# Four modulation vectors summed over the partitions: TensorE products against a GpSimd all-reduce

## The chip, the cores and the metric

The kernel runs on one core of a Trainium2 chip. The metric is the device time of one execution in microseconds; the time of a kernel is the median of its runs. Beside it stands one profiled execution, taken by the hardware profiler. Engines are named as the profile names them: PE is TensorE (PEld its weight loads), DVE is VectorE, ACT is ScalarE, POOL is GpSimd, SP is SyncE, which here issues most DMAs.

## The reference

A transformer block with adaptive layer norm: attention, then a gated MLP that mixes over the sequence. Six vectors of 448 elements come from one small product and scale and shift the two halves.

```
mod = silu(c) @ w_mod            # c is 1 x 448, w_mod 448 x (6 x 448)
sa, ca, ga, sb, cb, gb = mod     # six vectors of 448
h = layernorm(x) * (1 + ca) + sa
x = x + ga * attention(h, wqkv, wo)          # 16 heads of 28, 2048 rows
h = layernorm(x) * (1 + cb) + sb
z = gelu(h @ w_in); z1, z2 = halves of z; z2 = layernorm(z2)
x = x + gb * ((z1 * (w_sp @ z2 + b_sp)) @ w_out)
```

All data are single precision.

## The kernel before

Each large product is made in three terms: an operand is split into a part rounded to fp32r ("hi") and its remainder ("lo"), and hi x hi, hi x lo and lo x hi are summed in PSUM. The work goes in stages whose order is written out by hand; a semaphore waits wherever a tile, a buffer or a bank isn't free. Each engine, and the SP queue of DMA issues, works through its own instructions in the order of the program.

- **Start and projections (to some 83 us).** The rows of x go in four groups `g` of 512. For each group: `ln_transpose` (L104) transposes the normalised rows on PE, ACT scales and shifts them into `hfull`, rounds them into `hT`, and DVE subtracts to make the remainders; `v_tile` (L323) makes V; `qk_unit` (L329) makes 128 columns of Q or K for one group in 11 products, rounds the result into `qh`, subtracts for `ql`, and `qk_store` (L352) sends both to DRAM through SP. `qh`, `ql` and `qf` have two buffers each.
- **Preparation of the heads (group 3, L563 to L599).** `pads` (L572) fills parts of `kst` and `qst` for heads 0, 1 and 2, on DVE and POOL; `load_head` (L580) brings a head's Q and K back from DRAM through SP.
- **The ramp (L856 to L879).** The 18 remaining `qk_unit` calls run with the first products of the row maxima (`mt`, `m_mm`, L636) among their own. Here a unit is evacuated by ACT into `qf`, rounded into `qh`, and POOL subtracts for `ql` (L341 to L346). The units turn over three of the seven PSUM banks of the ring (L827 to L830), the `mt` products over the other four. The first six units are those of m = 4 for groups 0 to 3 and of m = 1 for groups 1 and 2.
- **Attention proper (to some 870 us), then the MLP.** PE makes scores, weighted sums and their like without a break.

**The vectors.** `sa` and `ca` are made at the start and the change doesn't touch them. The other four come in pairs, (ga, sb) as pair 1 and (cb, gb) as pair 2. `mod_acc` (L228) multiplies the rows of `w_mod` by silu(c) on DVE and adds them up in `acc`, 128 partitions by two times 448: what is left is a sum over the 128 partitions. `mod_split` (L245) makes hi and lo of `acc`: ACT rounds, and POOL (pair 1) or DVE (pair 2) subtracts. `mod_sum` (L256) multiplies each by a matrix of ones on PE, so that the sum stands in all 128 partitions of a bank. `mod_bc` (L263) copies it out (ga, gb); `mod_col` (L266) takes partition 0 as a row, adds 1 for cb, sends the row to DRAM and reads it back as columns by three DMAs, all through SP (sb, cb).

Pair 1 is accumulated among the products of group 1, split within group 3's `ln_transpose` (L552) and summed after `v_tile(11)` (L605, L606). Pair 2 is accumulated among the products of group 2, split after `v_tile(12)` (L595) and summed after `v_tile(15)` (L615, L616), just ahead of the ramp. In POOL's order, `pads` for heads 0, 1 and 2 come between the two pairs' sums, and the first `ql` of the ramp follows the second.

Of the kernel before, what the change touches and what calls it, by code (L numbers as in the profile page):

```python
# [1 line left out]

# [5 lines left out]

F32 = mybir.dt.float32
F32R = mybir.dt.float32r  # L10
AF = mybir.ActivationFunctionType
ALU = mybir.AluOpType
# [4 lines left out]
S, D, H, DH, FH = 2048, 448, 16, 28, 896  # L17
# [16 lines left out]
def tile_adaln_mha_gmlp(ctx, tc, x, wqkv, wo, w_in, w_spT, b_sp, w_out, cT, w_mod0, w_mod, out):  # L34
    nc = tc.nc
    ctx.enter_context(tc.manual_schedule())
    pe, dve, act, pool, sp = nc.tensor, nc.vector, nc.scalar, nc.gpsimd, nc.sync
# [3 lines left out]
    scr = ctx.enter_context(tc.tile_pool(name="scr", bufs=1, space=DRAM))  # L41
# [15 lines left out]
    cols = {}  # L57
    for nm in ("sa", "ca", "sb", "cb"):
        cols[nm] = const.tile([128, 4], F32, name=f"col_{nm}")
    bcs = {"gb": const.tile([128, D], F32, name="bc_gb")}  # L60
# [5 lines left out]
    def hview(heap, off, a, b):  # L66
        return heap[:, off : off + a * b].rearrange("p (a b) -> p a b", b=b)

    hT = [hview(heapD[g // 2], g % 2 * 3584, 7, 512) for g in range(NG)]
# [11 lines left out]
    def sub(eng, dst, a, hi):  # L81
        eng.tensor_tensor(out=dst, in0=a, in1=hi.bitcast(F32), op=ALU.subtract)  # L82
# [60 lines left out]
    stage = stg.enter_context(tc.tile_pool(name="stage", bufs=2, side="right"))  # L143
# [6 lines left out]
    e1 = early.enter_context(tc.tile_pool(name="e1", bufs=2))  # L150
    e2 = late_e.enter_context(tc.tile_pool(name="e2", bufs=1, side="right"))

    wv = e2.tile([128, 8, D], F32R, name="wv")
    ones_r = e2.tile([128, 128], F32R, name="ones_r")
    dve.memset(ones_r.bitcast(F32), 1.0)
    wms, xts, raws = {}, {}, {}


# [2 lines left out]
    def bank(name):  # L161
        k = mode[0](name) if mode[0] else banks[0]
        banks.remove(k)
        banks.append(k)
        return ring.tile([128, 512], F32, name=name, tag=f"b{k}")
# [52 lines left out]
    pc = bank("pc")  # L218
# [7 lines left out]
    accs = {}  # L226

    def mod_acc(pair, k):  # L228
        if k == 0:
            accs[pair] = e2.tile([128, 2, D], F32, name="acc")  # L230
        wm, acc = wms.pop((pair, k)), accs[pair]
        if k < 3:
            wm = wm.rearrange("r (p n) -> r p n", p=2)
        if k == 0:
            dve.tensor_scalar(out=acc, in0=wm, scalar1=silu[:, 0:1], scalar2=None, op0=ALU.mult)
        elif k < 3:
            dve.scalar_tensor_tensor(out=acc, in0=wm, scalar=silu[:, k : k + 1], in1=acc, op0=ALU.mult, op1=ALU.add)
        else:
            half_rows(wm, [acc[:, part] for part in range(2)])

    def half_rows(wm, outs):
        for part, o in enumerate(outs):
            dve.scalar_tensor_tensor(out=o, in0=wm, scalar=silu[:, 3 + part : 4 + part], in1=o, op0=ALU.mult, op1=ALU.add)

    def mod_split(pair, eng, pool_l, tag_l, bufs_l):  # L245

        acc = accs.pop(pair)
        accs[pair] = []
        for part in range(2):
            h = stage.tile([128, 512], F32R, name="acc_h", tag="qf")[:, :D]  # L250
            l = pool_l.tile([128, D], F32R, name="acc_l", tag=tag_l, bufs=bufs_l)
            act.activation(h, acc[:, part, :], AF.Copy)
            sub(eng, l, acc[:, part, :], h)
            accs[pair].append((h, l))

    def mod_sum(pair, part):  # L256

        pc = bank("pc")
        for i, a in enumerate(accs[pair][part]):
            pe.matmul(pc[:, :D], ones_r, a, start=i == 0, stop=i == 1)  # L260
        return pc[:, :D]

    def mod_bc(nm, pair, part):  # L263
        dve.tensor_copy(bcs[nm], mod_sum(pair, part))

    def mod_col(nm, pair, part, plus1):  # L266
        row, dst = e2.tile([1, D], F32, name="row"), scr.tile([D], F32, name=f"{nm}_scr")
        dve.tensor_scalar(out=row, in0=mod_sum(pair, part)[0:1], scalar1=plus1, scalar2=None, op0=ALU.add)
        sp.dma_start(dst.rearrange("(o n) -> o n", o=1), row)
        for r, e, c in ((0, 128, slice(0, 3)), (0, 64, slice(3, 4)), (64, 128, slice(3, 4))):  # L270
            src = dst[0:384] if e - r == 128 else dst[384:D]
            sp.dma_start(cols[nm][r:e, c], src.rearrange("(c p) -> p c", p=e - r))

    mv1, xn1 = {}, {}
# [13 lines left out]
    def ln_norm(g, ts):  # L288
        mv, rs = mv1[g]
        for t in ts:  # L290
            xn = e1.tile([128, 512], F32, name="xn", bufs=4)
            dve.tensor_scalar(
                out=xn[:, :D],
                in0=xts.pop(4 * g + t),
                scalar1=mv[:, t, 0:1],
                scalar2=rs[:, t : t + 1],
                op0=ALU.subtract,
                op1=ALU.mult,
            )
            act.activation(xn[:, D:], xn[:, 384:D], AF.Copy)  # L300
            xn1.setdefault(g, []).append(xn)
# [21 lines left out]
    def v_tile(kt):  # L323
        v_copy(*v_mm(kt))
# [212 lines left out]
    def ln_step(g, t):  # L537
        ln_stat(g, (t,))
        if t % 2:
            ln_rs(g, t - 1, t + 1)  # L540

    def ln_next(g):

        if g + 1 < NG:
            ln_transpose(
                xn1.pop(g), e1, hT[g], cols["ca"], cols["sa"], (act,) * 4, (dve,) * 4, None,
                lambda c: ln_step(g + 1, (0, 2, 1, 3).index(c)),
            )
            ln_norm(g + 1, range(4))
        else:  # L550
            ln_transpose(
                xn1.pop(g), e1, hT[g], cols["ca"], cols["sa"], (act,) * 4, (dve,) * 4, None, lambda c: c == 2 and mod_split(1, pool, e1, "wm", 4)  # L552
            )

    ln_next(1)
    load_x(3, sp)
    qk_unit((1,), 0)
# [4 lines left out]
    for g in range(1, NG):  # L562
        if g == 3:  # L563
            early.close()
            stk = att.enter_context(tc.tile_pool(name="stk", bufs=1))
            kq = [[stk.tile([128, S], F32R, name=f"{n}st{i}") for n in "kq"] for i in range(3)]
            kst, qst = [a[0] for a in kq], [a[1] for a in kq]
            npool = att.enter_context(tc.tile_pool(name="npool", bufs=2))
            late_s = ExitStack()
            late_l = late_s.enter_context(tc.tile_pool(name="late_l", bufs=2))  # L570

            def pads(i, eng):  # L572

                dve.memset(kst[i][64:128, :].bitcast(F32), 0.0)
                eng.memset(qst[i][64:128, :].bitcast(F32), 0.0)
                pool.memset(kst[i][64:86, :].bitcast(F32), 1.0)

            pads(0, dve)

            def load_head(h, c0=0, c1=S):  # L580
                k, q = kst[h % 3], qst[h % 3]
                if h > 2:
                    sp.dma_start(q[84:86, :].bitcast(F32), q[86:88, :].bitcast(F32))
                for r0, i in ((0, 0), (56, 1), (28, 0)):
                    sp.dma_start(k[r0 : r0 + 28, c0:c1].bitcast(F32), qk_scr[i][D + h * DH : D + (h + 1) * DH, c0:c1])
                for r0, i in ((0, 0), (28, 1), (56, 0)):
                    sp.dma_start(q[r0 : r0 + 28, c0:c1].bitcast(F32), qk_scr[i][h * DH : (h + 1) * DH, c0:c1])

            load_head(0, 0, 1536)
            for m in (0, 3):  # L590
                qk_unit((m,), g)
            load_head(0, 1536, S)
        v_tile(4 * g)
        if g == 3:
            mod_split(2, dve, late_l, "acc_l", 2)  # L595
        v_tile(4 * g + 1)
        if g == 3:
            pads(1, pool)
            pads(2, pool)  # L599
        if g + 1 < NG:  # L600
            ln_next(g + 1)
        for k in range(2):
            v_tile(4 * g + 2 + k)
            if g == 2 and k == 1:
                mod_bc("ga", 1, 0)  # L605
                mod_col("sb", 1, 1, 0.0)  # L606
            if g == 1 or g == 2 and k == 1:
                mod_acc(g, k if g == 1 else 0)
        if g < 3:
            for k, m in enumerate((0, 3)):  # L610
                qk_unit((m,), g)
                mod_acc(g, 3 - g + k)
            if g == 2:
                mod_acc(g, 3)
    mod_col("cb", 2, 0, 1.0)  # L615
    mod_bc("gb", 2, 1)  # L616
    late_s.close()
    late_e.close()


# [368 lines left out]
    h = H - 1  # L989
# [247 lines left out]
    acc = {}  # L1237
# [264 lines left out]
```

## Time and profile before

| what | value |
|---|---|
| median of 3 runs | 1396.14 us (1395.83 to 1396.7) |
| the profiled execution's own time | 1396.56 us |
| its span, first to last instruction | 1394.8 us |
| DMA queues with data | q1: 181.42 MB, q10: 4.30 MB, both hardware |
| instruction queues | q8: 0.92 MB, q14: 0.37 MB |
| granted TensorE clock, mean | 0.999 |

How to read it: the page's first part gives the busy time of each engine, its fourth the chain of work that ended last, its fifth groups of instructions by line (`out<-in`, count, busy time, mean in ns, and after the second bar the engine's idle time ahead of them with what ended it). A timeline row has the start and length in us, engine, line, operation, tiles and count. A row of a stretch (`a:b`) has its length, then the busy time and instructions of PE, PEld, DVE, ACT and POOL, then the granted clock, the DMA engines' busy share and GB/s. A row of the chain has the start, the length and what was on it.

### The profile page before, as it was taken

To read this page: it belongs to the slowest core of one execution; us is meant where nothing else is said; L and a number is where in the kernel's file an instruction comes from. 1 tells how busy PE (TensorE), PEld (TensorE's weight loads), DVE (VectorE), ACT (ScalarE), POOL (GpSimd) and SP (SyncE) were. 2 spreads that over 40 slices of the span, in tenths; PEclk is the share of its full clock that TensorE was granted. 3 is DMA by queue.
4 is the path that set the end of the run, shared out by engine and by line. 5 is a ranking of instruction groups with operands and counts; after the bars stand their busy time and mean duration, and the time that the engine had idled before them with its cause. 6 is when DMAs were issued, how large, how long until landed. Compare 5 with 4: busy or idle time off the path is not lost.

```text
span 1394.8 us, 20314 instructions
## 1 busy us (share of the span) xinstructions
PE 1389.4 (100%) x7170; PEld 989.0 (71%) x7170; DVE 1033.3 (74%) x1769; ACT 780.4 (56%) x1498; POOL 279.1 (20%) x279
## 2 busy tenths in 40 slices
PE   9999999999999999999999999999999999999998
PEld 8888655555555555555555555988998888888888
DVE  7898888888888888888888851750477655668573
ACT  6623677776666777777777778363244444334211
POOL 2134212222224143323200021000132430000000
PEclk9999999999999999999999999999999999999999
DMA  8464644665465556555323002434103333445453
GB/s 281 140 176 177 192 111 154 176 169 159 148 174 165 163 166 188 161 159 157 105 68 78 20 18 75 165 116 140 46 8 108 112 113 107 143 143 159 144 175 105
DMA packets 99489, 187.01 MB, mean 134 GB/s; under 512 B 17656, under 2 KB 29434, under 8 KB 96842
## 3 DMA queue, kind: packets, MB, share of 16 engines
q1 hardware_dynamic: 96670, 181.42, 43.3%
q10 hardware_dynamic: 2718, 4.30, 0.8%
q8 instruction: 56, 0.92, 0.3%
q14 instruction: 45, 0.37, 0.1%
HBM read 130.42 MB, written 50.46 MB: 130 GB/s over the span
## 4 chain that ended last, share of the span: by engine, by line
PE 98%; DVE 1%; DMA 0%; issue 0%; ACT 0%; ACTq 0%
PE st_ps L671 19%; PE o_ps L686 17%; PE mt L639 17%; PE acc L1246 7%; PE acc L1248 7%; PE acc L1247 7%; PE z_ps L1172 5%; PE pq L335 5%; PE z_ps L1058 5%; PE pv L317 2%; PE wo_ps L927 2%; PE y_ps L1353 2%; PE y_ps L1354 2%; PE y_ps L1352 2%; PE tp L111 1%; PE pv L464 0%
## 5 line engine op out<-in xcount | busy, mean ns | idle before, releaser
L644 DVE TENSOR_REDUCE pm<-mt 128x1 f32<-128x512 f32 x1024 | 631.1, 682 | 85.4 <-PE mt L639 85.4
L675 ACT ACTIVATE P<-st_ps 128x512 f32<-128x512 f32 x1024 | 514.7, 630 | 200.9 <-PE st_ps L671 200.9
L671 PE MATMUL st_ps<-qst,kst 128*128 128x512 f32 x1024 | 404.1, 406 | 0.0
L639 PE MATMUL mt<-kst,qst 128*128 128x512 f32 x1024 | 402.1, 393 | 0.0
L671 PEld LDWEIGHTS st_ps<-qst,kst 128*128 128x128 f32 x1024 | 191.2, 188 | 141.5 <-issue 93.1
L686 PE MATMUL o_ps<-P,V 128*32 128x512 f32 x2048 | 247.1, 598 | 0.0
L639 PEld LDWEIGHTS mt<-kst,qst 128*128 128x128 f32 x1024 | 192.4, 188 | 31.5
L790 POOL TENSOR_TENSOR ws_raw<-ws_raw 128x512 f32<-128x512 f32 x80 | 103.3, 1291 | 293.1 <-DMA ws_raw<-in_w_spT_dram 293.1
L1134 ACT ACTIVATE wsp_h<-raw_sp 128x512 fp32r<-128x512 f32 x112 | 70.1, 632 | 152.5 <-PE acc L1248 105.9
L82 DVE TENSOR_TENSOR wsp_l<-raw_sp,wsp_h 128x512 fp32r<-128x512 f32 x112 | 82.0, 743 | 81.0 <-ACT wsp_h L1134 80.3
L686 PEld LDWEIGHTS o_ps<-P,V 128*32 128x32 f32 x2048 | 54.6, 109 | 122.5 <-issue 114.3
L1246 PE MATMUL acc<-wsp_h,heapA 128*128 128x512 f32 x224 | 87.3, 390 | 0.0
L1247 PE MATMUL acc<-wsp_l,heapA 128*128 128x512 f32 x224 | 87.2, 389 | 0.0
L1248 PE MATMUL acc<-wsp_h,heapA 128*128 128x512 f32 x224 | 87.2, 389 | 0.0
L1247 PE MATMUL acc<-wsp_l,heapB 128*128 128x512 f32 x174 | 67.7, 389 | 0.0
L1246 PE MATMUL acc<-wsp_h,heapB 128*128 128x512 f32 x174 | 67.7, 389 | 0.0
L1248 PE MATMUL acc<-wsp_h,heapB 128*128 128x512 f32 x174 | 67.7, 389 | 0.0
L335 PE MATMUL pq<-heapD,heapD 128*128 128x512 f32 x196 | 61.8, 390 | 0.0
L1176 DVE BATCH_NORM_STATS2 stz<-z 128x6 f32<-128x448 f32 x32 | 19.8, 624 | 44.3 <-ACT z L1175 23.3
L1246 PEld LDWEIGHTS acc<-wsp_h,heapA 128*128 128x128 f32 x224 | 42.0, 188 | 8.9 <-DVE cD L1252 0.3
L1248 PEld LDWEIGHTS acc<-wsp_h,heapA 128*128 128x128 f32 x224 | 42.0, 188 | 8.9
L1247 PEld LDWEIGHTS acc<-wsp_l,heapA 128*128 128x128 f32 x224 | 42.0, 188 | 8.6
(225 smaller groups left out, 1601.4 us busy)
## 6 DMA issues: line engine op xcount, KB each, us to landing
ws_raw<-in_w_spT_dram SPq DMA_DIRECT2D x160, 256.0 KB
ws_scr<-ws_raw SPq DMA_DIRECT2D x80, 256.0 KB
raw_sp<-ws_scr SPq DMA_DIRECT2D x80, 256.0 KB
kst<-qk_scr SPq DMA_DIRECT2D x45, 224.0 KB
qst<-qk_scr SPq DMA_DIRECT2D x45, 224.0 KB
raw_sp<-in_w_spT_dram SPq DMA_DIRECT2D x32, 256.0 KB
qk_scr<-qh SPq DMA_DIRECT2D x28, 256.0 KB
qk_scr<-ql SPq DMA_DIRECT2D x28, 256.0 KB
```

Of the source, the lines that this page charges most:

```text
L82: eng.tensor_tensor(out=dst, in0=a, in1=hi.bitcast(F32), op=ALU.subtract)
L335: pe.matmul(pq, wqk[:, b, m * 128 : (m + 1) * 128], hT[g][:, a, :], start=j == 0, stop=j == NST - 1)
L639: pe.matmul(mt, qst[h % 3][:, t * 128 : (t + 1) * 128], kst[h % 3][:, kb * 512 : (kb + 1) * 512], start=True, stop=True)
L644: dve.tensor_reduce(out=pms[h][:, t, kb : kb + 1], in_=mt, axis=AX.X, op=ALU.max)
L671: pe.matmul(st, kst[h % 3][:, kt * 128 : (kt + 1) * 128], qst[h % 3][:, qb * 512 : (qb + 1) * 512], start=True, stop=True)
L675: act.activation(p, st, AF.Exp, scale=SCALE)
L686: pe.matmul(otile[h][32 * qb : 32 * qb + 32, :], V[:, kt, h, :], ptiles.pop((u, qb)), start=kt == 0, stop=kt == NT - 1)
L790: pool.tensor_tensor(out=a, in0=a, in1=b, op=SUMS[i // 16][2])
L1134: act.activation(hi, raw, AF.Copy)
L1246: pe.matmul(acc[i], zh, hi, start=st == 0, stop=False)
L1247: pe.matmul(acc[i], zh, lo, start=False, stop=False)
L1248: pe.matmul(acc[i], zl, hi, start=False, stop=st == 7)
```

## The change

The sum over the partitions is made by POOL's all-reduce from `acc` itself, without a split, straight into its destination; the result stands in all partitions. For cb the 1 is then added on POOL to partition 0 of the row; for sb nothing is added. `mod_split`, the matrix of ones `ones_r` and the remainders' tiles go. `acc` and `row` get two buffers, `row` now has 128 partitions, and the area kept for descriptors of POOL's DMAs is cut to 4096 bytes a partition to make room. The accumulation, the DMAs and the places of `mod_bc` and `mod_col` in the program stay.

```diff
-    ones_r = e2.tile([128, 128], F32R, name="ones_r")
-    dve.memset(ones_r.bitcast(F32), 1.0)
...
-            accs[pair] = e2.tile([128, 2, D], F32, name="acc")
+            accs[pair] = e2.tile([128, 2, D], F32, name="acc", bufs=2)
...
-    def mod_split(pair, eng, pool_l, tag_l, bufs_l):
-
-        acc = accs.pop(pair)
-        accs[pair] = []
-        for part in range(2):
-            h = stage.tile([128, 512], F32R, name="acc_h", tag="qf")[:, :D]
-            l = pool_l.tile([128, D], F32R, name="acc_l", tag=tag_l, bufs=bufs_l)
-            act.activation(h, acc[:, part, :], AF.Copy)
-            sub(eng, l, acc[:, part, :], h)
-            accs[pair].append((h, l))
-
-    def mod_sum(pair, part):
-
-        pc = bank("pc")
-        for i, a in enumerate(accs[pair][part]):
-            pe.matmul(pc[:, :D], ones_r, a, start=i == 0, stop=i == 1)
-        return pc[:, :D]
+    def mod_sum(pair, part, out):
+
+        pool.partition_all_reduce(out, accs[pair][:, part, :], 128, bass_isa.ReduceOp.add)
 
     def mod_bc(nm, pair, part):
-        dve.tensor_copy(bcs[nm], mod_sum(pair, part))
+        mod_sum(pair, part, bcs[nm])
 
     def mod_col(nm, pair, part, plus1):
-        row, dst = e2.tile([1, D], F32, name="row"), scr.tile([D], F32, name=f"{nm}_scr")
-        dve.tensor_scalar(out=row, in0=mod_sum(pair, part)[0:1], scalar1=plus1, scalar2=None, op0=ALU.add)
-        sp.dma_start(dst.rearrange("(o n) -> o n", o=1), row)
+        row, dst = e2.tile([128, D], F32, name="row", bufs=2), scr.tile([D], F32, name=f"{nm}_scr")
+        mod_sum(pair, part, row)
+        if plus1:
+            pool.tensor_scalar(out=row[0:1], in0=row[0:1], scalar1=plus1, scalar2=None, op0=ALU.add)
+        sp.dma_start(dst.rearrange("(o n) -> o n", o=1), row[0:1])
...
-                xn1.pop(g), e1, hT[g], cols["ca"], cols["sa"], (act,) * 4, (dve,) * 4, None, lambda c: c == 2 and mod_split(1, pool, e1, "wm", 4)
-            )
+                xn1.pop(g), e1, hT[g], cols["ca"], cols["sa"], (act,) * 4, (dve,) * 4)
...
-        if g == 3:
-            mod_split(2, dve, late_l, "acc_l", 2)
...
-    nc = _bacc.Bacc("TRN2", target_bir_lowering=False, num_devices=1)
+    nc = _bacc.Bacc("TRN2", target_bir_lowering=False, num_devices=1, dynamic_dma_scratch_size=4096)
```

More of the change, by code (lines that the diff above doesn't have):

```diff
@@ L4 @@
 import concourse.tile as tile
-from concourse import mybir
+from concourse import bass_isa, mybir
 from concourse.masks import make_identity
@@ L568, in tile_adaln_mha_gmlp @@
             npool = att.enter_context(tc.tile_pool(name="npool", bufs=2))
-            late_s = ExitStack()
-            late_l = late_s.enter_context(tc.tile_pool(name="late_l", bufs=2))
             def pads(i, eng):
@@ L616, in tile_adaln_mha_gmlp @@
     mod_bc("gb", 2, 1)
-    late_s.close()
     late_e.close()
```

## The prediction

> **What bounds the kernel now.** I read the page first: busy time by engine, then the chain that ended last.
>
> ```profile
> PE 1389.4 (100%) x7170; PEld 989.0 (71%) x7170; DVE 1033.3 (74%) x1769; ACT 780.4 (56%) x1498; POOL 279.1 (20%) x279
> PE 98%; DVE 1%; DMA 0%; issue 0%; ACT 0%; ACTq 0%
> ```
>
> TensorE is busy all the time and is 98% of the chain. So a microsecond in which TensorE waits is a microsecond of the result, and work taken from another engine gains nothing unless TensorE waits for it. POOL, which gets the new work, is 80% idle as a mean, but what counts is its idle time at the place. Hence two more views: the stretches around the change, then the chain in order of time.
>
> ```profile
> 86.00:102.00 16.00, 16.00 (x73) 13.23 (x72) 15.14 (x24) 3.80 (x7) 3.25 (x3) 1.00 0.65 170
> 102.00:118.00 16.00, 16.00 (x72) 13.27 (x71) 14.31 (x21) 7.21 (x12) 8.54 (x7) 1.00 0.59 203
> ```
>
> ```profile
> 62.73 0.81 PE pc L260 x4
> 82.48 0.81 PE pc L260 x4
> ```
>
> From 86 to 118 us TensorE (first number after the length) is full and its clock is 1.00. The products that the change removes stand on the chain twice, 0.81 us each.
>
> **The change part by part.** *Removed.* Eight products: 2 x 0.81 = 1.62 us of TensorE, all of it on the path. The rest was beside it: the roundings and row copies below, and POOL's share of the remainders.
>
> ```profile
> L252 ACT ACTIVATE acc_h<-acc 128x448 fp32r<-128x448 f32 x4 | 2.1, 568 | 0.0
> L82 DVE TENSOR_TENSOR acc_l<-acc,acc_h 128x448 fp32r<-128x448 f32 x2 | 1.2, 618 | 0.0
> L268 DVE TENSOR_SCALAR row<-pc 1x448 f32<-1x448 f32 x2 | 1.2, 607 | 0.0
> L82 POOL TENSOR_TENSOR acc_l<-acc,acc_h 128x448 fp32r<-128x448 f32 x2 | 2.4, 1200 | 8.0 <-ACT acc_h L252 8.0
> ```
>
> TensorE never waited for these, so I cost them at nothing. The second accumulator buffer takes away a wait that isn't seen. The smaller descriptor scratch touches no transfer here, since every queue of data on the page is a hardware one. Rows and accumulators now live until POOL has read them, but the P tiles that can take their place come only with the attention proper.
>
> *Added.* Four all-reduces over 128x448 on POOL, and one addition of 1 on a row. Their price isn't in the trace. Nearest rows:
>
> ```profile
> L102 POOL TENSOR_TENSOR rs<-rs,mhalf 128x2 f32<-128x2 f32 x6 | 5.5, 916 | 25.9 <-DVE rs L101 23.8 <-DMA wm<-in_w_mod_dram 2.1
> L102 POOL TENSOR_TENSOR rs<-rs,mhalf 128x4 f32<-128x4 f32 x5 | 5.5, 1092 | 45.0 <-DVE rs L101 39.1 <-ACT z1t L1062 6.0
> L653 POOL TENSOR_SCALAR mxv<-mxv 128x16 f32<-128x16 f32 x16 | 4.1, 254 | 93.8 <-DVE mxv L651 93.8
> L82 POOL TENSOR_TENSOR mxp<-mxv,mxp 128x16 fp32r<-128x16 f32 x16 | 3.6, 226 | 1.4
> ```
>
> One all-reduce, d: at least one pass over the tile, 1.2 us (the remainder row above). Seven halvings of 128 partitions at a pass each make 8.4 us. A software loop like the power is far dearer: 1.092 us / 4 = 0.273 us a column, 122 us for 448; by the step from two to four columns, 0.088 us a column, about 40 us. I take the middle of one and seven passes, **d = 4.8 us**, since a sum is nearer to an addition than to a power, and keep 1.2 and 122 as ends. The addition of 1: 0.254 us at 16 columns plus what a two-input operation gains from 16 to 448 columns (1.200 - 0.226) makes 1.2 us; ends 0.6 (DVE's row) and 0.254 / 16 x 448 = 7.1.
>
> *Code.* No all-reduce has run on POOL before, and its program may not lie beside that of the tensor operations. If so, POOL must change programs wherever the two kinds alternate: before the first sum, between the third sum and the addition of 1, between that and the fourth sum, and before the next subtraction. No row shows such a change, R. Code does come by DMA (first row), so I bound it by transfers of this stretch, zero being the lower end.
>
> ```profile
> q8 instruction: 56, 0.92, 0.3%
> ```
>
> ```profile
> 87.97 0.26 SPq L269 DMA_DIRECT2D cb_scr<-row  x1
> 89.38 1.56 SPq L272 DMA_DIRECT2D col_cb<-cb_scr  x3
> 94.76 0.34 SPq L354 DMA_DIRECT2D qk_scr<-qh  x1
> 101.28 0.63 ACT L345 ACTIVATE qh<-qf 128x512 fp32r<-128x512 f32 x1 [6.39 <-DMA qk_scr<-qh]
> ```
>
> A row of 1.8 KB needs 89.38 - 87.97 = 1.4 us from issue until its reader is issued; a 256 KB store, behind others, 101.28 - 94.76 = 6.5 us. A program is nearer in size to the second: **R = 6.5 us**, ends 0 and 6.5. The Trainium skill (GPSIMD Engine Reference, section 2.1 Instruction dispatch) says that POOL's kernels are loadable and that the first call of a freshly loaded one pays about 6 us; by it the sum below would be 1.5 us less, and no run here shows it.
>
> *First pair of sums (ga, sb).*
>
> ```profile
> 51.42 0.90 POOL L102 TENSOR_TENSOR rs<-rs,mhalf 128x2 f32<-128x2 f32 x1 [2.08 <-DMA wm<-in_w_mod_dram]
> 57.26 1.27 DVE L243 SCALAR_TENSOR_TENSOR acc<-wm,silu,acc 128x448 f32<-128x448 f32 x2
> 59.77 0.69 DVE L82 TENSOR_TENSOR heapD<-hfull,heapD 128x512 fp32r<-128x512 f32 x1 [0.64 <-ACT heapD L125]
> 60.29 2.35 POOL L82 TENSOR_TENSOR acc_l<-acc,acc_h 128x448 fp32r<-128x448 f32 x2 [7.96 <-ACT acc_h L252]
> 62.05 1.14 DVE L82 TENSOR_TENSOR heapD<-hfull,heapD 128x512 fp32r<-128x512 f32 x1 [1.58 <-ACT heapD L125]
> 65.28 0.29 SPq L269 DMA_DIRECT2D sb_scr<-row  x1
> 68.57 0.60 ACT L348 ACTIVATE qh<-pq 128x512 fp32r<-128x512 f32 x1 [1.89 <-PE pq L335]
> 71.06 0.60 ACT L348 ACTIVATE qh<-pq 128x512 fp32r<-128x512 f32 x1 [1.89 <-PE pq L335]
> 74.72 1.80 POOL L576 MEMSET kst<- 22x2048 f32 x1 [12.08 <-ACT qh L348]
> 76.55 0.74 SPq L585 DMA_DIRECT2D kst<-qk_scr  x2
> ```
>
> POOL is free from 52.3 us, the accumulator is done at 58.5. The first code change hides in that gap (if it waits for the accumulator it costs 6.5 us here). The sums end at 58.6 + 2 x 4.8 = 68.2 us; the SP queue, in which sb_scr stands at 65.28, is held 2.9 us, and behind it the stores of two projection units and head 0's loads. Those loads wait for POOL's fill of kst at 76.5 anyway, which is the cover.
>
> One thing speaks against the change here: the DVE subtraction at 62.05 took 1.14 us, against 0.69 for the same operation at 59.77, while POOL's remainders (60.29 to 62.64) ran. So DVE with two SBUF operands and POOL stand in each other's way. With POOL reading until 68.2 us, the three subtractions that make hT's remainders, due from 59.8, can slip to 68.2 + 3 x 0.69 = 70.3 us. The projection unit that reads them starts when the one ahead ends (68.57, less 0.81 for the products) and takes 2.5 us (71.06 - 68.57), so TensorE wants them from about its middle, 69 us: some 1 us of stall, which the later wait below swallows, and the second accumulator and the fills of kst/qst up to 3.7 us later. The Trainium skill (SBUF — State Buffer, Who interferes with whom) calls the shared port an exclusive lock for the whole instruction; the 1.14 us agree. By a shared port instead of a lock, POOL's fills would not move and the sum would be 3 us less.
>
> *Second pair (cb, gb): what decides.*
>
> ```profile
> 84.87 1.80 POOL L576 MEMSET kst<- 22x2048 f32 x1
> 88.37 1.30 POOL L82 TENSOR_TENSOR ql<-qf,qh 128x512 fp32r<-128x512 f32 x1 [1.70 <-issue]
> 94.28 0.60 ACT L341 ACTIVATE qf<-pq 128x512 f32<-128x512 f32 x1 [2.42 <-PE pq L335]
> 105.17 0.60 ACT L341 ACTIVATE qf<-pq 128x512 f32<-128x512 f32 x1 [0.19 <-PE pq L335]
> ```
>
> In POOL's queue this pair stands behind the fills for heads 1 and 2 (the last ends at 86.7 us) and ahead of the subtraction that makes ql of the first ramp unit (88.37). Today they are 1.7 us apart. Less the DVE remainders (1.2 us) and products (0.8) that went, the fills would end at about 85 us; with most of the slip above, at about **88 us**. Then:
>
> 88 + 4.8 (sum) + 6.5 + 1.2 (plus 1) + 6.5 + 4.8 (sum) + 6.5 = 118.3 us, and the first ql runs to 119.6.
>
> Who waits: qf has two buffers, so the third unit's qf (today 94.28) needs the first unit's subtraction; it runs from 119.7 to 120.3. The ramp units turn over three PSUM banks, so the sixth unit takes the third's and can't start before 120.4. Today the sixth unit's products end at 105.17, and a unit takes 3.63 us (from 94.28 to 105.17 are three units), so it starts at 101.54. Difference: **18.9 us**, with the 1.62 us of products already in it, since the start is set by POOL and not by TensorE. cb_scr waits in the SP queue until about 100.5 (12.5 us late), and behind it head 1's loads and all stores of the ramp; these come free before ql does, so they add nothing of their own. Nothing returns afterwards: TensorE is full to the end.
>
> *Clock.* A stall that long may cost clock as well. At the start of the kernel, where TensorE's work is thin:
>
> ```profile
> 8.00:10.00 2.00, 1.93 (x15) 1.84 (x15) 1.78 (x6) 0.96 (x4) 0.90 (x1) 0.81 1.06 404
> 10.00:12.00 2.00, 2.00 (x11) 2.00 (x10) 1.93 (x8) 0.98 (x3) 0.00 (x0) 0.50 1.07 419
> 12.00:14.00 2.00, 2.00 (x13) 1.94 (x12) 0.85 (x5) 1.31 (x3) 0.00 (x0) 0.83 0.98 389
> ```
>
> The granted clock there costs 2 x (0.19 + 0.50 + 0.17) = 1.7 us. I add 1.7 (ends 0 and 1.7).
>
> **Sum.** 18.9 + 1.7 = 20.6 us on the profiled execution's 1396.56 us (span 1394.8 us, 1.8 us around it), which is 0.4 us over the median of 1396.14: **1417 us**. Ends of the terms: with d = 1.2 and R = 6.5 and fills ending at 85, the first ql would end at 85 + 2.4 + 19.5 + 1.2 + 1.3 = 109.4 and the sixth unit start at 110.2: 1396.56 + 8.7 + 1.7 = 1407. With d = 8.4 and R = 6.5 the slips grow (fills to 94): ql to 94 + 16.8 + 19.5 + 1.2 + 1.3 = 132.8, start 133.6, 1430. With d = 8.4 and R = 1.4 it is 15.3 less, 1415. Each further microsecond of d costs two on POOL and about two more by the slip, so some 1440 stands at d = 10.5.
>
> **The rivals.** *1. Not slower: POOL's gap is wide enough.* Place: POOL between the last fill and the sixth unit's start. Without the products the sixth unit would start at 99.9, so the chain from the fills' end at 85 has 14.9 us; less 1.3, 1.2 and 0.8 for the subtraction, the addition and the third qf, 2d + 3R up to 11.6 us is free. With no code change that holds up to about d = 5. Then only the products count: 1396.56 - 1.62 = 1395 us. For it: POOL is 80% idle and ACT already sat 6.4 us in this stretch without TensorE noticing. Against it: only 1.7 us separate the fill from ql, and three code changes alone overdraw it. Faster than 1.62 us it cannot be.
>
> *2. The sum is a software loop of tens of microseconds.* By the power's step of 0.088 us a column, d = 40: the first pair ends at 138.6 us, the fills some 20 us later (as today, from 65.28 to 86.7), and the sixth unit starts at 158.6 + 80 (two sums) + 19.5 (three code changes) + 3.3 (addition, subtraction, qf) = 261.4, which is 160 us late: with the clock 1558 us. For it: POOL's only non-streaming row, the power. Against it: an addition needs no such loop. The Trainium skill (GPSIMD Engine Reference, section 3.2) gives 247.7 us for a reduction over partitions of [128, 2048], an estimate of 54 us for 448 columns; no run here shows this instruction.
>
> **How the numbers follow.** Forecast (POOL's second pair with code changes or longer sums holds the ramp, 1398 to 1440) 0.80; rival 1 0.10; rival 2, with all beyond 1440, 0.10. The range 1398 to 1440 leaves out 0.20. 0.2% is 2.8 us, about what a measurement of this kernel can tell. Rival 1 gives no change (0.09; 0.01 faster), the others are slower: 0.90.
>
> **What would show it.** Right: in the profile after, TensorE idle time inside one ramp unit near 100 to 120 us released by ACT's qf, ACT's qf released by POOL's ql, gaps on POOL on both sides of the row's addition of 1, and cb_scr some 10 us late. The first pair costs little if sb_scr is issued near 68 us. Wrong: POOL operations back to back without gaps (R is nothing), a sum of more than 10 us, or a stall at the first mt products (83 us) larger than that of the ramp, which would put the cost with the first pair and DVE.

## The result and the profile after

The changed kernel takes 1412.24 us (median of 4 runs, 1411.16 to 1413.38), the kernel before 1396.42 us beside it: a ratio of 1.0113, 95% interval 1.01 to 1.0125. It is slower by 15.8 us; 1417 us was forecast, with 1398 to 1440 as the range.

The page of the changed kernel, its first line, first part and fourth part:

```profile
span 1409.9 us, 20284 instructions
PE 1390.9 (99%) x7162; PEld 988.0 (70%) x7162; DVE 1032.3 (73%) x1762; ACT 779.8 (55%) x1494; POOL 289.7 (21%) x282
PE 91%; issue 2%; DVE 1%; DMA 1%; POOL 0%; SPq 0%; ACT 0%; POOLq 0%; DVEq 0%
```

TensorE's busy time is nearly what it was (1389.4 before), but the span grew by 15.1 us: TensorE waits now, and the chain holds 2% of "issue", time in which an engine waited for nothing that the profile shows. The stretches of the changed kernel say where:

```profile
86.00:102.00 16.00, 13.34 (x59) 10.70 (x57) 12.97 (x20) 1.37 (x3) 3.36 (x3) 1.00 0.23 55
102.00:118.00 16.00, 5.23 (x12) 4.13 (x13) 2.21 (x4) 3.55 (x6) 6.60 (x5) 0.50 0.54 151
118.00:134.00 16.00, 16.00 (x70) 13.15 (x69) 13.48 (x20) 5.23 (x9) 6.45 (x5) 0.97 0.48 172
```

Before, TensorE was full in all of these. Now it is idle for 2.7 us of the first and 10.8 us of the second, where its granted clock is 0.50 besides. Outside the ramp no loss of this size is seen (0.41 us at its first mt product, below). The waits of the changed kernel from 50 to 150 us (who waited for whom: total, times, longest) and POOL's timeline give the reason:

```profile
ACT qf L327 <- POOL ql L82: 22.4, 1, 22.4
PE pq L321 <- ACT qf L327: 13.4, 1, 13.4
POOL ql L82 <- issue: 7.3, 1, 7.3
POOL row L254 <- issue: 6.8, 1, 6.8
POOL bc_gb L245 <- issue: 5.8, 1, 5.8
```

```profile
56.94 3.21 POOL L245 PARTITION_ALL_REDUCE bc_ga<-acc  x1 [5.75 <-DVE acc L241]
60.07 3.03 POOL L245 PARTITION_ALL_REDUCE row<-acc  x1
...
81.90 1.81 POOL L559 MEMSET kst<- 22x2048 f32 x1
83.80 2.87 POOL L245 PARTITION_ALL_REDUCE row<-acc  x1
93.47 1.36 POOL L254 TENSOR_SCALAR row<-row 1x448 f32<-1x448 f32 x1 [6.79 <-issue]
100.67 2.89 POOL L245 PARTITION_ALL_REDUCE bc_gb<-acc  x1 [5.84 <-issue]
110.83 2.49 POOL L82 TENSOR_TENSOR ql<-qf,qh 128x512 fp32r<-128x512 f32 x2 [7.27 <-issue]
```

A sum takes 2.9 to 3.2 us. Between the second pair's sums and the tensor operations stand three gaps, 6.8, 5.8 and 7.3 us, in which POOL waits for no other engine. They make 19.9 us; the two sums and the addition of 1 make 7.1. Two instructions of POOL's sequencer stand at the start of each gap, and a fourth pair ahead of the first sum, at 51.2 us (source lines of the changed kernel; L254's at 86.6 us, the last at 103.5):

```profile
L245 POOLq MODIFY_POOL_CONFIG  x4: 1/4/6, 51.2 to 95.1; - x4
L254 POOLq MODIFY_POOL_CONFIG  x2: 87/88/88, 86.6 to 86.7; - x2
L82 POOLq MODIFY_POOL_CONFIG  x2: 98/98/98, 103.5 to 103.5; - x2
```

So POOL changes its program four times, at each passage between all-reduce and tensor operation. (That it is a program is read from the name and the place of these two; what POOL does in the gap, no row shows.) The fills (MEMSET) need no change: the third sum starts 0.1 us behind the last of them. The chain runs as forecast: ql of the first unit, then the third unit's qf (22.4 us of waiting), then its bank, then the sixth unit, which starts after 13.4 us of idle TensorE:

```profile
98.72 0.61 PE L321 MATMUL pq<-heapD,heapF 128*128 128x512 f32 x2
112.77 0.79 PE L321 MATMUL pq<-heapD,heapD 128*128 128x512 f32 x1 [13.43 <-ACT qf L327]
```

In the kernel before, the sixth unit's first product stands here:

```profile
101.28 0.39 PE L335 MATMUL pq<-heapD,heapD 128*128 128x512 f32 x1
```

### The profile page after: what moved, and what is told of

It reads as the page before. It is cut to its first block, busy times and chain, and to the rows that moved or that the text cites. A ratio compares the mean times of both kernels' runs of the same rounds, so it can differ in the third digit from the quotient of the medians.

```text
span 1409.9 us, 20284 instructions
## 1 busy us (share of the span) xinstructions
PE 1390.9 (99%) x7162; PEld 988.0 (70%) x7162; DVE 1032.3 (73%) x1762; ACT 779.8 (55%) x1494; POOL 289.7 (21%) x282
## 4 chain that ended last, share of the span: by engine, by line
PE 91%; issue 2%; DVE 1%; DMA 1%; POOL 0%; SPq 0%; ACT 0%; POOLq 0%; DVEq 0%
PE st_ps L651 18%; PE o_ps L666 17%; PE mt L619 16%; PE acc L1228 6%; PE acc L1227 6%; PE acc L1226 6%; PE z_ps L1152 5%; PE z_ps L1038 5%; PE pq L321 2%; PE wo_ps L907 2%; PE y_ps L1333 2%; PE y_ps L1332 2%; PE y_ps L1334 2%; PE tp L111 1%; DMA qk_scr<-ql 0%
## 5 line engine op out<-in xcount | busy, mean ns | idle before, releaser
L651 PEld LDWEIGHTS st_ps<-qst,kst 128*128 128x128 f32 x1024 | 191.2, 187 | 141.8 <-issue 93.1
L321 PE MATMUL pq<-heapD,heapD 128*128 128x512 f32 x196 | 63.6, 400 | 13.4 <-ACT qf L327 13.4
L321 PEld LDWEIGHTS pq<-heapD,heapD 128*128 128x128 f32 x196 | 37.7, 193 | 21.6 <-ACT qf L327 13.9
```

The costliest lines, as they stand in the source:

```text
L321: pe.matmul(pq, wqk[:, b, m * 128 : (m + 1) * 128], hT[g][:, a, :], start=j == 0, stop=j == NST - 1)
L651: pe.matmul(st, kst[h % 3][:, kt * 128 : (kt + 1) * 128], qst[h % 3][:, qb * 512 : (qb + 1) * 512], start=True, stop=True)
```

## The experiments

Each ratio is against the kernel before, measured in the same round: 1395.53 us for experiments 1, 2, 4 and 7, 1396.13 us for 3, 5, 6 and 8. Code that stays or that only repeats the edit elsewhere is left out at `...`.

**1. The addition of 1 taken off POOL.** The 1 is added to cb's columns later, on DVE:

```diff
-        if plus1:
-            pool.tensor_scalar(out=row[0:1], in0=row[0:1], scalar1=plus1, scalar2=None, op0=ALU.add)
...
+    def cb_plus():
+        dve.tensor_scalar(out=cols["cb"], in0=cols["cb"], scalar1=1.0, scalar2=None, op0=ALU.add)
+
+    at(60, cb_plus)
```

> The 1 is added to cb's columns on DVE, late in the attention, so that on POOL the third and fourth sums stand next to each other. Theory 1 (changing POOL's program between the kinds is what costs): the gaps of 6.8 and 5.8 us around the addition vanish, the second sum of the pair starts within 0.3 us of the first one's end, one gap of about 7 us stays ahead of the first ql, which ends near 98 us instead of 112.1; the sixth ramp unit starts near 99.5 us without a wait and the kernel takes 1394.5 to 1396.5 us, as the kernel before or a little less. Theory 2 (the gaps are the hidden end of the sums themselves, which take some 9 us each): a gap of about 6 us stays between the two sums, the first ql ends near 104 us, the sixth unit starts some 3 us late, its clock drops, and the kernel takes 1399 to 1403 us.

Measured: 1395.02 us, beside 1395.53 for the kernel before (ratio 0.9995, interval 0.9986 to 1.0003). POOL's timeline of this kernel, then TensorE's sixth unit:

```profile
83.89 2.88 POOL L245 PARTITION_ALL_REDUCE row<-acc  x1
86.67 2.95 POOL L245 PARTITION_ALL_REDUCE bc_gb<-acc  x1
97.75 2.52 POOL L82 TENSOR_TENSOR ql<-qf,qh 128x512 fp32r<-128x512 f32 x2 [8.12 <-issue]
```

```profile
99.71 0.50 PE L319 MATMUL pq<-heapD,heapD 128*128 128x512 f32 x1 [0.21 <-ACT qf L325]
```

Two sums side by side have no gap between them; the whole loss is gone with one addition over a row of 448. The sixth unit waits 0.21 us. This settles theory 1 against theory 2: a sum ends where the profile says, and the gap belongs to the passage from one kind of operation to the other. It also shows that both pairs of sums can be had on POOL at the time of the kernel before, not measurably under it.

**2. gb summed first, the addition behind both sums.**

```diff
+    mod_bc("gb", 2, 1)
     mod_col("cb", 2, 0, 1.0)
-    mod_bc("gb", 2, 1)
```

> gb is summed ahead of cb, with the addition of 1 left on POOL behind both sums: one change of program ahead of the addition, none between it and ql. Theory 1 with POOL alone counting: the first ql ends at about 83.8 + 2.9 + 2.9 + 6.8 + 1.4 + 1.3 = 99 us, the sixth unit isn't late, 1395 to 1397 us. Theory 3 (the SP queue, held by the row of cb, counts by itself): cb_scr is issued only at about 98 us, the first unit's store at about 103, its buffer comes free at 106 or later, and the seventh unit, due at 103, waits some 3 us for its bank: 1399 to 1401 us. Theory 2 (hidden ends of the sums): first ql at 105 us or later, 1400 us and more.

Measured: 1406.74 us (ratio 1.0078, 1.0064 to 1.0092). POOL did what theory 1 said, yet the loss is 11 us, at least twice what theory 3 was given. Three views of this kernel, POOL's, ACT's and SP's timelines:

```profile
98.01 1.36 POOL L254 TENSOR_SCALAR row<-row 1x448 f32<-1x448 f32 x1 [6.92 <-issue]
99.36 2.52 POOL L82 TENSOR_TENSOR ql<-qf,qh 128x512 fp32r<-128x512 f32 x2
```

```profile
100.67 0.60 ACT L327 ACTIVATE qf<-pq 128x512 f32<-128x512 f32 x1 [9.18 <-POOL ql L82]
112.16 0.63 ACT L331 ACTIVATE qh<-qf 128x512 fp32r<-128x512 f32 x1 [10.89 <-DMA qk_scr<-qh]
```

```profile
99.40 0.21 SPq L255 DMA_DIRECT2D cb_scr<-row  x1
...
104.92 0.34 SPq L340 DMA_DIRECT2D qk_scr<-qh  x1
```

ql comes in time (100.6 us). But the SP queue stands at cb's row until 99.4, then issues the loads of cb's columns and of head 1, and only at 104.9 the first unit's store. Its buffer comes free 7.2 us later (112.16), the third unit's qh waits 10.9 us for it, and the seventh unit starts 8.1 us late, at half the clock again. The 3 us expected here were too few: the store was issued 1.9 us later than expected, and it took 7.2 us until its buffer was free and not 3 (6.5 in the kernel before).

**3. The same, with cb's DMAs late.** To see whether it was the SP queue, the row keeps its own buffer and its four DMAs (now in `to_cols`) are issued in the attention:

```diff
...
+        if nm == "sb":
+            to_cols()
+        else:
+            cb_cols.append(to_cols)
...
+    at(41, cb_late)
```

> As the run with gb summed first (1406.74 us), but the four DMAs of cb (row to DRAM, three loads of columns) are issued late in the attention, so that the row no longer holds the SP queue. Theory 3 (there the SP queue, held to 99.4 us, made the loss of 11 us: the third unit's qh waited 10.9 us for the first unit's store): the first unit's stores are issued near 91 to 95 us, that wait shrinks to a few microseconds, the seventh unit isn't late, and the kernel takes 1395 to 1397 us. Rival (the loss there came from POOL, the addition of 1 and one change of program): it stays above 1402 us.

Measured: 1396.61 us (ratio 1.0006, 0.9996 to 1.0015). SP's and ACT's timelines:

```profile
89.44 0.34 SPq L347 DMA_DIRECT2D qk_scr<-qh  x1
```

```profile
101.37 0.63 ACT L338 ACTIVATE qh<-qf 128x512 fp32r<-128x512 f32 x1
104.78 0.63 ACT L338 ACTIVATE qh<-qf 128x512 fp32r<-128x512 f32 x1 [2.21 <-DMA qk_scr<-qh]
```

The first unit's store is issued at 89.44 us, and the third unit's qh (101.37) doesn't wait any more; in experiment 2 it waited 10.9 us. The longest wait for a store is now 2.21 us, at the fourth unit's qh. So a row that POOL makes late has two prices: what follows it on POOL, and what follows its DMA in the SP queue. In the changed kernel the second (store at 100.37) was hidden under the first (ql at 112.1).

**4. Only ga and sb on POOL.** cb and gb are split and summed by TensorE as in the kernel before:

```diff
...
+        if pair == 1:
+            pool.partition_all_reduce(row, accs[pair][:, part, :], 128, bass_isa.ReduceOp.add)
+        else:
+            dve.tensor_scalar(out=row[0:1], in0=mod_sum(pair, part)[0:1], scalar1=plus1, scalar2=None, op0=ALU.add)
...
```

> Only ga and sb are summed on POOL; cb and gb stay with the products of ones, as before. Theory 1: the one change of program back to the tensor operations falls between the fills and the first ql (91 to 95 us instead of 88.4), which the three banks and two buffers cover; 0.8 us of products are gone; 1395.3 to 1396.5 us. Rival (the first pair costs, since DVE and POOL stand in each other's way and the SP queue is held): TensorE waits between 59 and 83 us for hT's remainders or head 0's loads, and the kernel takes 1398 us or more.

Measured: 1394.95 us beside 1395.53 (ratio 0.9997, 0.9988 to 1.0006). POOL's first ql:

```profile
93.09 2.54 POOL L82 TENSOR_TENSOR ql<-qf,qh 128x512 fp32r<-128x512 f32 x2 [7.20 <-issue]
```

TensorE is full from 58 to 102 us. The change back to tensor operations is issued behind the fills and takes 7.2 us, up to a first ql at 93.1, and costs nothing there. The first pair is free.

**5. The sums made small.** All four over 32 of the 448 columns; the kernel leaves out the other 416:

```diff
-        pool.partition_all_reduce(out, accs[pair][:, part, :], 128, bass_isa.ReduceOp.add)
+        dve.memset(out, 0.0)
+        pool.partition_all_reduce(out[:, 0:32], accs[pair][:, part, 0:32], 128, bass_isa.ReduceOp.add)
```

> The changed kernel with all four sums over 32 of the 448 columns; the other columns of the four vectors are left at zero, so that part of the computation is left out. Theory 1 (the three changes of POOL's program make the loss, the sums only their own 2.9 us each): the gaps of 6.8, 5.8 and 7.3 us stay, the two sums of the second pair shrink to under 0.6 us each, the first ql ends 4.5 to 5 us earlier (near 107 us) and the kernel takes about 5 us less than the changed kernel, 1406.5 to 1408.5 us. Theory 2 (the gaps belong to the sums and go with their size): the gaps shrink as well and the kernel comes to within 2 us of the kernel before.

Measured: 1407.03 us (ratio 1.0079, 1.0062 to 1.0096).

```profile
83.70 0.53 POOL L246 PARTITION_ALL_REDUCE row<-acc  x1
91.88 1.36 POOL L255 TENSOR_SCALAR row<-row 1x448 f32<-1x448 f32 x1 [7.65 <-issue]
99.44 0.55 POOL L246 PARTITION_ALL_REDUCE bc_gb<-acc  x1 [6.20 <-DVE pm L625]
107.60 2.48 POOL L82 TENSOR_TENSOR ql<-qf,qh 128x512 fp32r<-128x512 f32 x2 [7.61 <-issue]
```

With almost nothing left of the sums, the gaps stay (7.65, 6.20, 7.61 us) and 10.9 us of the loss with them. The 6.20 is put down to a DVE reduction here; it is the same gap, since two MODIFY_POOL_CONFIG stand at its start (the second at 93.5 us). Between this span and that of the changed kernel lie 4.9 us: the two sums were 4.7 us shorter, the three gaps 1.6 us longer, so the first ql ended 3.2 us earlier (108.8 against 112.1), and the shorter wait cost 1.2 us less of clock. 0.5 us isn't assigned.

**6. The sums of the second pair made twice,** on top of experiment 1 (`pair` is 1 or 2, so the first pair stays as it was):

```diff
...
+        for _ in range(pair):
+            mod_sum(pair, part, row)
```

> As the run with the 1 added late (1395.02 us), with each sum of the second pair made twice, 5.7 us more of POOL's time with no further change of program. Theory 1 with the slack worked out (some 14 us of POOL's time behind the last fill are free, and that run has used them up): each further microsecond counts; the first ql ends near 104.7 us, the sixth unit starts 5 to 6 us late, with 1 to 2.5 us of clock on top: 1401 to 1403.5 us. Rival (a wait of a few microseconds is taken up elsewhere, by the free banks): below 1398 us.

Measured: 1404.38 us (ratio 1.0058, 1.0043 to 1.0073), 0.9 over the expected stretch. POOL's timeline of this kernel and TensorE's sixth unit:

```profile
84.04 5.84 POOL L245 PARTITION_ALL_REDUCE row<-acc  x2
89.78 5.92 POOL L245 PARTITION_ALL_REDUCE bc_gb<-acc  x2
104.72 2.48 POOL L82 TENSOR_TENSOR ql<-qf,qh 128x512 fp32r<-128x512 f32 x2 [9.02 <-issue]
```

```profile
106.65 0.79 PE L321 MATMUL pq<-heapD,heapD 128*128 128x512 f32 x1 [7.36 <-ACT qf L327]
```

ql starts 7.0 us later than in experiment 1 (104.72 against 97.75: 5.9 of sums, 0.9 of a longer program change, 0.2 elsewhere), and the sixth unit 6.9 us later (106.65 against 99.71). The slack is used up in experiment 1, and from there each microsecond on POOL is one on TensorE. Of the 9.0 us between the two spans the clock makes 1.6: TensorE's work ran at 0.50 for some 3.2 us, from 106.65 until the clock came back near 109.9 (0.55 from 109 to 110 us, 1.00 after it). 0.5 us isn't assigned.

**7 and 8. TensorE kept busy in the wait.** Products of the identity by ones, ahead of the sixth unit of the changed kernel, 64 and then 56 of them:

```diff
+        if i == 5:
+            fill = ps_o.tile([128, 512], F32, name="fill", tag="o")
+            for _ in range(64):
+                pe.matmul(fill[:, 0:128], ident, ones, start=True, stop=True)
```

> The changed kernel with 64 products of the identity by ones into a free bank, whose result nobody reads, put ahead of the sixth ramp unit, about as long as its wait. Theory 4 (part of the loss is clock: the granted clock fell to 0.50 during the wait and stayed there for the sixth and part of the seventh unit): the clock stays at 1.00, the sixth unit takes 3.6 us instead of 6.6, and the kernel takes about 3 us less than the changed kernel, 1408.5 to 1410 us. Rival (the slow unit comes from the late data, not from the clock): no gain, 1412 us.

> As the run with 64 filler products (1409.26 us), whose filler ended 1.2 us after the data were there, with 56 of them, which end at about 112.4 us. Theory 4 (clock): the sixth unit starts at 112.8 us as in the changed kernel, at clock 1.00, and the kernel takes 1408 to 1409 us, some 3.5 us less than the changed kernel. Rival (the gain of 3 us was something else): no less than 1409.3 us.

Measured: 1409.26 us (ratio 1.01, 1.0087 to 1.0114) and 1408.42 us (ratio 1.0086, 1.0071 to 1.0101). The stretch from 102 to 118 us with 64 of them:

```profile
102.00:118.00 16.00, 16.00 (x128) 15.30 (x127) 3.31 (x5) 3.28 (x6) 7.28 (x5) 1.00 0.57 156
```

The clock is 1.00 where the changed kernel had 0.50. The sixth unit with 56 of them:

```profile
113.72 0.50 PE L321 MATMUL pq<-heapD,heapD 128*128 128x512 f32 x1 [1.82 <-ACT qf L327]
```

With 56 the filler ended early enough, but POOL's program changes took 1 us more in that run and the sixth unit started at 113.72 instead of 112.77; its span is 2.3 us shorter all the same. So some 3 us of the loss are clock and the rest is the wait.

## Why the prediction was right

The mechanism was the forecast one: POOL's second pair with three program changes delays the first ql, and by two buffers and three banks the sixth unit. Term by term:

- **One sum:** 4.8 us forecast, 2.9 measured (3.2 for the first). Mis-sized by 1.9 us, twice on the path. By experiment 5 the cost is (2.89 - 0.55) / (448 - 32), 5.6 ns a column, and about 0.4 us besides. The figure of 54 us that was worked out from the Trainium skill (GPSIMD Engine Reference, section 3.2) for a reduction over partitions doesn't hold for this instruction: the runs show about a nineteenth.
- **Program changes:** 3 x 6.5 = 19.5 us forecast, 6.8 + 5.8 + 7.3 = 19.9 measured. Where the changes fall was reasoned; that they need 6.6 us each and the forecast said 6.5 is luck. The 6.5 was borrowed from a 256 KB store, and the instruction queues carry the same (q8 0.92 MB, q14 0.37 MB) with the changes as without, so no row shows a program come by DMA. That the fills between the pairs need no change was assumed without a word; one more ahead of the third sum would, as an estimate from these gaps, have put some 6 us more on the path. Over all runs a change took 5.8 to 9.0 us; the Trainium skill's 6 us (the same page, section 2.1) is near the lower end. The first hid in POOL's idle time, as assumed: issued at 51.2, the sum began at 56.9 when the accumulator was ready.
- **The addition of 1:** 1.2 forecast, 1.36 measured.
- **The slip of the fills:** the step that failed. They were to end at 88 us and ended at 83.7, about the 85 forecast without a slip, less the 1.1 us by which this execution was ahead (below). DVE's subtractions were held up by POOL, but until 63.4 us and not 70.3, ahead of the need at 69 us. The shorter sums (ended at 63.1 instead of 68.2) make 5.1 us of that. The rest is that not all three subtractions waited for the end of both sums: each sum held up one (last section). The fills came out as by the prediction's other reading, a shared port without a lock, by which they wouldn't move. TensorE was full from 58 to 74 us, and experiment 4 shows the first pair at no cost.
- **The first ql's end:** 119.6 forecast, 112.1 measured, early by the 4.3 us of the fills and 3.8 of the two sums, less the 0.4 and 0.2 that came on top.
- **The sixth unit's start:** +18.9 us forecast, 112.77 - 101.28 = +11.5 measured. (The prediction worked out 101.54 for the kernel before; the trace has the first product at 101.28.) About 1.1 us of the difference is a better start of that profiled execution (POOL's power operation stands at 47.22 against 48.34 before the change has begun), not the change: in experiments 2 and 3, whose program is the same up to there, it stands at 48.77 and 48.17.
- **Clock:** 1.7 us forecast, 3.0 measured. From its first product to the start of its qf the sixth unit took 6.9 us (112.77 to 119.64) instead of 3.9 (101.28 to 105.17). The start-up, from which the 1.7 came, was a shorter dip.
- **Products:** 1.62 us forecast, as a saving within the start of the sixth unit. In the changed kernel TensorE stands 0.41 us at the first mt product, so some 1.2 us were had; in experiments 1 (all of the products gone) and 4 (half of them), where this is the only thing left, the medians gain 0.5 and 0.6 us, within their intervals of no change.

The sum by the profile: 11.5 + 3.0 = 14.5, and the span grew by 15.1; 0.6 us isn't assigned. 20.6 was forecast, too high by the sums and the slip, in part made good by the clock.

Rival 1 (POOL's gap is wide enough) had its bound right: 2d + 3R up to 11.6 us with the addition on POOL, against 25.7 measured. Experiment 1, with 2d + R = 13.9 us and no addition (which widens the bound to 12.8), sits about at that edge with 0.21 us of waiting. Rival 2 (tens of microseconds a sum) is out.

## What to carry to other kernels

Price an instruction of GpSimd by its neighbours in GpSimd's queue: in this kernel a passage between the all-reduce and a tensor operation cost 6 to 9 us each way, two to three times the sum of 448 columns itself. Keep the odd kind together, move small tensor operations between its instructions to another engine, and place the passages where the queue is idle: the same four sums then cost nothing that could be measured. Look also at what stands behind a late result in the DMA queue.

## What the runs showed of the hardware

POOL and DVE stood in each other's way more than the page lets one see, though here at no cost. DVE's timeline around the first pair, in the changed kernel and in experiment 5, whose sums ran only later:

```profile
57.32 2.44 DVE L82 TENSOR_TENSOR heapD<-hfull,heapD 128x512 fp32r<-128x512 f32 x1
59.69 0.68 DVE L82 TENSOR_TENSOR heapD<-hfull,heapD 128x512 fp32r<-128x512 f32 x1
61.27 1.45 DVE L82 TENSOR_TENSOR heapD<-hfull,heapD 128x512 fp32r<-128x512 f32 x1 [0.91 <-ACT heapD L125]
62.76 0.69 DVE L82 TENSOR_TENSOR heapD<-hfull,heapD 64x512 fp32r<-64x512 f32 x1
```

```profile
57.24 0.68 DVE L82 TENSOR_TENSOR heapD<-hfull,heapD 128x512 fp32r<-128x512 f32 x1
58.53 0.69 DVE L82 TENSOR_TENSOR heapD<-hfull,heapD 128x512 fp32r<-128x512 f32 x1 [0.60 <-ACT heapD L125]
```

A subtraction that needs 0.69 us took 2.44 and 1.45 us where an all-reduce ran beside it: busy time on DVE can be waiting. The Trainium skill (SBUF — State Buffer, Who interferes with whom) has this as a lock for the whole instruction. The waits agree with a lock, but not with one up to the recorded end of the sum: the next subtraction ran in its usual time from 59.69 and from 62.76 us, while the sums are recorded until 60.15 and 63.10. Whether the lock was given up early or the record ends late, no run here tells.

The clock's fall and return in the changed kernel, in stretches of 1 us:

```profile
101.00:102.00 1.00, 0.00 (x0) 0.00 (x0) 0.00 (x0) 0.00 (x0) 1.00 (x1) 0.93 0.88 213
118.00:119.00 1.00, 1.00 (x4) 0.75 (x3) 0.56 (x1) 0.00 (x0) 0.37 (x1) 0.54 0.47 166
```

TensorE ran dry at 99.3 us, and the clock fell to 0.50 near 101.9 (0.93 is the mean of that stretch); work began again at 112.8, and the clock was back near 118.9 (0.54). Read in the same way, in this kernel and in experiments 2, 5 and 6 it fell 2.5 to 3.8 us after TensorE ran dry and was back 3.2 to 6.2 us after work began, so the same kind of wait cost 1.6 to 3.1 us of clock. A program change took between 5.8 and 9.0 us from run to run. What decides either wasn't tried.
